# One rotation of four PSUM banks for up products and everything else in a two-branch transformer block

## The chip, the cores and the metric

The kernel runs on one core of one Trainium2 chip. The metric is device time in microseconds (us) of one execution. A core has a matmul engine (TensorE, PE in the profile, with its weight loads as PEld), VectorE (DVE), ScalarE (ACT), GpSimd (POOL) and SyncE (SP), which issues most DMAs. Each engine takes its instructions strictly in the order in which they stand in its queue, and waits on semaphores that other engines or DMAs raise. Matmul results land in PSUM, which has eight banks of 128 partitions x 512 fp32. A bank can be written again only when what it held has been read out by ACT or DVE.

## What is computed

Input x is 2048 tokens x 512. Two branches read it, and a gate mixes them:

```python
g = sigmoid((x * gate_w).sum(-1, keepdims=True))
q, k, v = split_heads(x @ wqkv)                      # 32 heads of 16
phi(t) = concat(softmax(t @ w_phi), softmax(-t @ w_phi))
kv, z  = phi(k)^T v, sum over tokens of phi(k)       # linear attention
a      = (phi(q) kv / (phi(q) z + 1e-6)) @ wo
b      = relu(x @ w1 + b1)**2 @ w2 + b2              # 512 -> 1792 -> 512
out    = g * a + (1 - g) * b
```

## The kernel before

**Numbers.** Each fp32 operand is split into a high part (`..h`, rounded to the matmul's fp32r type by ACT) and a low part (`..l`, the rest, by DVE): `split`, L59. A product is then three matmuls per 128 rows of contraction (`mm3`, L67: high x high, high x low, low x high), so a product of 128 x 512 outputs over a contraction of 512 is 12 matmuls of 512 columns, 4 at L69, 4 at L70 and 4 at L71.

**Blocks.** Tokens are taken in 4 blocks of 512 (`SB`), each of 4 chunks of 128. The hidden size is cut into 14 slices of 128, 7 per sweep, in 2 sweeps over the 4 blocks: 56 steps t. A step has an up product u (hidden slice x block, transposed, `up`, L312), an ACT relu, square and split (`hidden`, L303), and two steps later four down products d, one per chunk (`down`, L318), which accumulate over the 7 slices in the four banks of `ps_d`.

**Attention work between the steps.** The first sweep also computes keys k and values v of all chunks (`do_k`, L402, `do_v`, L408), whose 16 pairs add up the key sums `kvps` (`do_kv`, L413) in one bank. The second computes queries q, their features, transposes by DMA, the numerators `num` (`numer`, L265) and the attended rows `att`. Before keys and before queries, w_phi is folded into the weights, 16 small matmuls in pairs of four (`fold`, L139: `foldk`, `foldq`), whose result is split from PSUM into `wkh`, `wkl` (or `wqh`, `wql`). A table of slots (`at`, L469), two per step, says after which up or down products these pieces are issued in the program. From that program order, priorities and dependencies a scheduler sets each engine's queue before the run.

**PSUM before.** Four banks are `ps_d`. Two are `ps_u`, used alternately by up products. The last two, `ps_a` and `ps_b`, are taken in turn by `bank()` (L51) for folds, k, v, q, num, att and the transposed sums `kvt`. After the fourth key fold `do_fold` drops `ps_b` out of the turn (L331), because `do_kv` keeps the key sums there until `kv_done` (L428) puts it back: in that stretch k and v share the single bank `ps_a`. A k is read out of its bank by four DVE instructions (L200 to L203, `exps`), a v by one ACT copy (L411, `vext`), an up product by one ACT relu (L305), a fold by ACT (L61) and then DVE (L64).

**Loads.** SP issues the loads in program order. Weights and x pass through four staging buffers (`in`), each free again after its split. x rows for the gate (`row<-in_xn`, L171), the broadcast bias `b2b` (L473) and the gate weights `gwb` (L472) are loaded in the same queue.

Of the kernel before, what the change touches and what calls it, by code (L numbers as in the profile page):

```python
# [8 lines left out]
F32 = mybir.dt.float32  # L9
# [4 lines left out]
PSUM = bass.MemoryType.PSUM  # L14
DRAM = bass.MemoryType.DRAM

P = 128
S, D, H, DH, F = 2048, 512, 32, 16, 1792
NK = D // P
SB = 512  # L20
# [12 lines left out]
def tile_gated_mix(ctx: ExitStack, tc: tile.TileContext, xT, xn, wqT, wkT, wphi, wv, wo, w1, b1, w2, b2, gw, out):  # L33
    nc = tc.nc
    pool = lambda name, bufs, **kw: ctx.enter_context(tc.tile_pool(name=name, bufs=bufs, **kw))
# [6 lines left out]
    small = pool("small", 3)  # L42
    dram = pool("dram", 1, space=DRAM)
    ps_d = pool("ps_d", NC, space=PSUM)
    ps_u = pool("ps_u", 2, space=PSUM)
    ps_a = pool("ps_a", 1, space=PSUM)
    ps_b = pool("ps_b", 1, space=PSUM)
    banks = [ps_a, ps_b]
    taken = [0]

    def bank(name):  # L51
        p = banks[taken[0] % len(banks)]
        taken[0] += 1
        return p.tile([P, 512], F32, tag="s", name=name)
# [4 lines left out]
    def split(src, hi, lo, ehi, elo):  # L59
        if ehi is nc.scalar:  # L60
            i = nc.scalar.activation(hi, src, AF.Copy)  # L61
        else:
            i = ehi.tensor_copy(hi, src)
        elo.tensor_tensor(lo, src, hi.bitcast(F32), ALU.subtract)  # L64
        return i
# [11 lines left out]
    def load(src):  # L77
        t = stage.tile([P, 512], F32, tag="in", name="in")
        nc.sync.dma_start(t, src)
        return t  # L80

    def row():
        return work.tile([P, D], F32, tag="row", name="row", bufs=6)

    def ffn_tiles(nm, fc):
        return (fpool.tile([P, 512], F32R, tag=nm + "h", name=f"{nm}h{fc}"),
                fpool.tile([P, 512], F32R, tag=nm + "l", name=f"{nm}l{fc}"))
# [51 lines left out]
    def fold(loaded, nm, k):  # L139
        wph, *t = loaded  # L140
        ps = bank(f"fold{nm}{k}")
        for g in range(NK):
            nc.tensor.matmul(ps[:, g * P:(g + 1) * P], t[g][:, k * P:(k + 1) * P], wph[:, g * P:(g + 1) * P],
                             start=True, stop=True)
        hi = wpool.tile([P, 512], F32R, tag=f"wah{k}", name=f"w{nm}h{k}")
        lo = wpool.tile([P, 512], F32R, tag=f"wal{k}", name=f"w{nm}l{k}")
        with tc.high_priority(offset=AHEAD):
            split(ps, hi, lo, nc.scalar, nc.vector)
        return hi, lo
# [150 lines left out]
    def up_step(ps, k, xs, wf):  # L300
        st["up"] = mm3(ps, wf, xs[k], slice(k * P, (k + 1) * P), ALL, k == 0, k == NK - 1)

    def hidden(fc, ps):  # L303
        r = work.tile([P, SB], F32, tag="r", name="r")
        nc.scalar.activation(r, ps, AF.Relu, bias=b1c[:, fc:fc + 1])  # L305
        nc.scalar.activation(r, r, AF.Square)  # L306
        hh = work.tile([P, SB], F32R, tag="hh", name="hh", bufs=LAG + 1)
        hl = work.tile([P, SB], F32R, tag="hl", name="hl", bufs=LAG + 1)
        st["act"] = split(r, hh, hl, nc.scalar, nc.vector)
        return hh, hl  # L310

    def up(fc, xs, wf):  # L312
        ps = ps_u.tile([P, SB], F32, tag="u", name="u")
        for k in range(NK):
            up_step(ps, k, xs, wf)
        return hidden(fc, ps)
# [8 lines left out]
    def do_fold(nm, k):  # L325
        with tc.issue_after(st["up"].ins):
            st["wa", nm, k] = fold(st["wT"], nm, k)
        if k == NK - 1:
            st["wa"] = [st["wa", nm, i] for i in range(NK)]
            if nm == "k":  # L330
                banks.pop()  # L331

    def do_w(src, nm):
        st["wb"] = load_w(src, nm)
# [23 lines left out]
    def idle(n):  # L358
        for _ in range(n):
            st["up"] = nc.tensor.matmul(st["warm"], st["zeros"][:, :P], st["zeros"], start=True, stop=True)  # L360


    def start():
        t = row()
        hi, lo = up_w[0] = ffn_tiles("w1", 0)
        xs = st["x", 0] = []
        ps = ps_u.tile([P, SB], F32, tag="u", name="u")
        for k in range(NK):
            s = slice(0, P) if k == 0 else slice(P, 512)
            u = load(xT[0, :, k, :])  # L370
            if k == 0:
                for piece in (s, slice(P, 512)):
                    nc.scalar.dma_start(t[:, piece], w1[0][:, piece])
            xs.append((xpool.tile([P, SB], F32R, tag="xh", name=f"xh0_{k}"),
                       xpool.tile([P, SB], F32R, tag="xl", name=f"xl0_{k}")))
            if k == 0:
                split(t[:, s], hi[:, s], lo[:, s], nc.vector, nc.vector)
            nc.scalar.activation(xs[k][0], u, AF.Copy)
            low = nc.vector.tensor_tensor(xs[k][1], u, xs[k][0].bitcast(F32), ALU.subtract)
            if k == 0:  # L380
                rest_w = slice(P, 512)
                with tc.issue_after(low.ins):
                    split(t[:, rest_w], hi[:, rest_w], lo[:, rest_w], nc.vector, nc.gpsimd)
            (xh, xl), kk = xs[k], slice(k * P, (k + 1) * P)
            with tc.issue_after(st["up"].ins):
                st["up"] = nc.tensor.matmul(ps, hi[:, kk], xh, start=k == 0, stop=False)
            if k < 2:
                with tc.issue_after(st["up"].ins):
                    idle(2)
            with tc.issue_after(st["up"].ins):  # L390
                nc.tensor.matmul(ps, hi[:, kk], xl, start=False, stop=False)
                st["up"] = nc.tensor.matmul(ps, lo[:, kk], xh, start=False, stop=k == NK - 1)
            if k < 1:
                with tc.issue_after(st["up"].ins):
                    idle(2)
        st["u0"] = ps
# [81 lines left out]
    for k in range(NK):  # L478
        at(3 + k // 2, do_fold, "k", k)
    at(1, do_w, wv, "v")  # L480
    for b in range(NB):
        for c in range(NC):
            s = b * SL + 3 * c - 3 if b else 7 + c
# [3 lines left out]
        for c in range(NC):  # L487
            n = b * NC + c
            s = 5 + 2.9 * n
# [6 lines left out]
    for k in range(NK):  # L496
        at(49 + k, do_fold, "q", k)
# [7 lines left out]
    for p in range(NB * NC // 2):  # L505
        n, s = 2 * p, 54 + 6 * p
# [12 lines left out]
    def do_up(t):  # L519
        if t < len(work_list):  # L520
            sw, b, i = work_list[t]
            fc = sw * NFH + i
            hid[t] = up(fc, st["x", sw * NB + b], up_w[fc])

    warm_up()
    start()
    for fc in range(1, LAG + 1):
        do_w1(fc)
# [87 lines left out]
```

## Time and profile before

| | us |
|---|---|
| median of 3 runs | 531.09 |
| lowest, highest | 531.03, 531.55 |
| span of the profiled execution | 528.2 |

The span goes from the first to the last instruction of one profiled execution. The timed runs hold some 2.9 us more around it. In the timeline a row is: start us, length us, engine, line, operation, out<-in, matmul size, shape, count; in brackets stands the idle time before it and what ended it. A matmul's length overlaps the next one's, so the distance from one start to the next is what a matmul costs on a busy PE.

### The profile page before, as it was taken

How to read it: one execution, taken by the hardware profiler on the slowest of the kernel's cores; microseconds unless marked ns; L12 is line 12 of the kernel's file. 1: busy time of each engine (PE TensorE's matmuls, PEld its weight loads, DVE VectorE, ACT ScalarE, POOL GpSimd, SP SyncE). 2: the span in 40 equal slices, each digit the busy share in tenths (PEclk: the TensorE clock that was granted, in tenths of full speed). 3: DMA queues.
4: the chain of work that ended last, by engine and by line, in shares of the span. 5: the costliest groups of instructions: out<-in, count | busy, mean ns of one | idle time of the engine just before them, and what ended most of it. 6: DMA issues, size and time to landing. Idle time of an engine off the chain costs nothing.

```text
span 528.2 us, 8945 instructions
## 1 busy us (share of the span) xinstructions
PE 519.0 (98%) x3475; PEld 417.6 (79%) x3475; DVE 356.5 (68%) x608; ACT 234.1 (44%) x404; POOL 77.0 (15%) x61
## 2 busy tenths in 40 slices
PE   8998999999999999999999999999999999999997
PEld 4876888888888888888878878787887878787785
DVE  4688546833656334566769897998878887779423
ACT  4874424623335234354644663463435353535230
POOL 2001111111111111011103121102011111112000
PEclk9999999999999999999999999999999999999999
DMA  7974004200032000434346114134102311022102
GB/s 255 297 234 131 1 1 161 81 2 1 24 138 79 2 0 22 159 85 137 81 146 215 34 40 124 66 107 130 45 17 89 113 49 30 24 77 94 47 1 79
DMA packets 30834, 45.16 MB, mean 86 GB/s; under 512 B 5704, under 2 KB 12360, under 8 KB 30792
## 3 DMA queue, kind: packets, MB, share of 16 engines
q1 hardware_dynamic: 30328, 44.20, 26.8%
q8 instruction: 27, 0.44, 0.4%
q10 hardware_dynamic: 432, 0.39, 0.2%
q14 instruction: 15, 0.12, 0.1%
q0 software_dynamic: 32, 0.01, 0.0%
HBM read 29.89 MB, written 8.39 MB: 72 GB/s over the span
## 4 chain that ended last, share of the span: by engine, by line
PE 63%; DVE 15%; DMA 7%; ACT 5%; SPq 5%; issue 2%; POOL 2%; DVEq 0%; POOLq 0%; ACTq 0%
PE u L69 6%; PE u L71 6%; PE u L70 6%; PE d L71 6%; PE d L70 6%; PE d L69 6%; SPq L259 4%; PE k L69 3%; PE v L69 2%; PE k L70 2%; PE k L71 2%; PE v L70 2%; PE v L71 2%; DMA in<-in_w 2%; PE att L69 2%
## 5 line engine op out<-in xcount | busy, mean ns | idle before, releaser
L305 ACT ACTIVATE r<-u,b1c 128x512 f32<-128x512 f32 x56 | 38.5, 687 | 152.1 <-PE u L71 143.5
L69 PE MATMUL d<-w2h,hh 128*128 128x512 f32 x224 | 87.5, 390 | 0.0
L69 PE MATMUL u<-xh,w1h 128*128 128x512 f32 x220 | 86.8, 395 | 0.4 <-ACT w1h L61 0.4
L70 PE MATMUL d<-w2l,hh 128*128 128x512 f32 x224 | 87.2, 389 | 0.0
L71 PE MATMUL d<-w2h,hl 128*128 128x512 f32 x224 | 87.2, 389 | 0.0
L71 PE MATMUL u<-xh,w1l 128*128 128x512 f32 x220 | 85.8, 390 | 0.1
L70 PE MATMUL u<-xl,w1h 128*128 128x512 f32 x220 | 85.7, 390 | 0.0
L64 DVE TENSOR_TENSOR hl<-r,hh 128x512 fp32r<-128x512 f32 x56 | 42.8, 764 | 55.9 <-ACT hh L61 55.9
L233 POOL TENSOR_TENSOR ez<-e,z 128x512 f32<-128x512 f32 x32 | 41.4, 1316 | 187.7 <-ACT e L205 187.7
L214 POOL TENSOR_TENSOR e<-e,r 128x1024 f32<-128x1024 f32 x16 | 32.4, 2025 | 202.1 <-DVE r L210 144.8
L208 DVE TENSOR_REDUCE sm<-e 128x64 f32<-128x1024 f32 x32 | 39.0, 1217 | 28.5 <-ACT e L205 28.3
L69 PEld LDWEIGHTS u<-xh,w1h 128*128 128x128 f32 x220 | 41.3, 188 | 12.2 <-ACT hh L61 1.6
L71 PEld LDWEIGHTS d<-w2h,hl 128*128 128x128 f32 x224 | 42.1, 188 | 8.7
L69 PEld LDWEIGHTS d<-w2h,hh 128*128 128x128 f32 x224 | 42.0, 188 | 8.7
L70 PEld LDWEIGHTS d<-w2l,hh 128*128 128x128 f32 x224 | 42.1, 188 | 8.6
L71 PEld LDWEIGHTS u<-xh,w1l 128*128 128x128 f32 x220 | 41.3, 188 | 9.1 <-DVE w1l L64 0.6
L70 PEld LDWEIGHTS u<-xl,w1h 128*128 128x128 f32 x220 | 41.3, 188 | 8.2
L205 ACT ACTIVATE e<-e 128x1024 f32<-128x1024 f32 x32 | 33.8, 1055 | 23.2 <-DVE e L203 22.4
L257 ACT ACTIVATE phiT<-tb 32x256 f32<-32x256 f32 x64 | 26.4, 413 | 34.6 <-DVE tb L251 33.9
L61 ACT ACTIVATE hh<-r 128x512 fp32r<-128x512 f32 x56 | 35.2, 628 | 1.3
L306 ACT ACTIVATE r<-r 128x512 f32<-128x512 f32 x56 | 35.1, 627 | 1.0
L566 DVE SCALAR_TENSOR_TENSOR row<-d,rest,row 128x512 f32<-128x512 f32 (+1 forms) x33 | 22.4, 731 | 8.5 <-PE d L71 8.5
(106 smaller groups left out, 875.4 us busy)
## 6 DMA issues: line engine op xcount, KB each, us to landing
in<-in_xT SPq DMA_DIRECT2D x32, 256.0 KB, 3.8
in<-in_w SPq DMA_DIRECT2D x24, 256.0 KB, 3.1
phiT<-tb SPq DMA_DIRECT2D x192, 32.0 KB, 1.8
row<-in_xn SPq DMA_DIRECT2D x16, 256.0 KB, 2.8
part<-row SPq DMA_DIRECT2D x16, 256.0 KB, 2.0
row<-part SPq DMA_DIRECT2D x16, 256.0 KB, 3.7
out<-row SPq DMA_DIRECT2D x15, 256.0 KB, 2.3
row<-in_wkT SPq DMA_DIRECT2D x4, 256.0 KB, 5.8
```

What stands on the lines that cost most here:

```text
L61: i = nc.scalar.activation(hi, src, AF.Copy)
L64: elo.tensor_tensor(lo, src, hi.bitcast(F32), ALU.subtract)
L69: nc.tensor.matmul(o, ah[:, sa], bh[:, sb], start=first, stop=False)
L70: nc.tensor.matmul(o, ah[:, sa], bl[:, sb], start=False, stop=False)
L71: return nc.tensor.matmul(o, al[:, sa], bh[:, sb], start=False, stop=last)
L205: nc.scalar.activation(ef, ef, AF.Exp)
L208: nc.vector.tensor_reduce(sm, e3, AX.X, ALU.add)
L214: eng.tensor_tensor(e3, e3, w.unsqueeze(2).to_broadcast([P, 2 * H, DH]), ALU.mult)
L233: nc.gpsimd.tensor_tensor(ez[:, hs, :], e3[:, hs, :], zbc[half], ALU.mult)
L257: nc.scalar.activation(dst, src, AF.Copy)
L305: nc.scalar.activation(r, ps, AF.Relu, bias=b1c[:, fc:fc + 1])
L306: nc.scalar.activation(r, r, AF.Square)
```

## The change

The two up banks and the two banks of the rest become one list of four, `[ps_a, ps_b, ps_e, ps_f]`, and up products take theirs from `bank()` like everything else. The first up product, u of slice 0, is given `ps_e` outright and does not count in the turn. While the key sums hold `ps_b`, the list has three banks.

```diff
     ps_d = pool("ps_d", NC, space=PSUM)
-    ps_u = pool("ps_u", 2, space=PSUM)
-    ps_a = pool("ps_a", 1, space=PSUM)
-    ps_b = pool("ps_b", 1, space=PSUM)
-    banks = [ps_a, ps_b]
+    ps_a, ps_b, ps_e, ps_f = (pool(f"ps_{i}", 1, space=PSUM) for i in "abef")
+    banks = [ps_a, ps_b, ps_e, ps_f]
...
     def up(fc, xs, wf):
-        ps = ps_u.tile([P, SB], F32, tag="u", name="u")
+        ps = bank("u")
...
             if nm == "k":
-                banks.pop()
+                banks.remove(ps_b)
...
         xs = st["x", 0] = []
-        ps = ps_u.tile([P, SB], F32, tag="u", name="u")
+        ps = ps_e.tile([P, SB], F32, tag="s", name="u")
```

By the program order, takes 0 to 6 of the new turn are u1, u2, u3, foldk0, foldk1, foldk2, foldk3 in a, b, e, f, a, b, e. Then `ps_b` leaves, and take 7 modulo 3 is e again: u4 stands in the bank of foldk3. Takes 8 to 12 are k0 in f, u5 in a, v0 in e, k1 in f, u6 in a.

The scheduler answers with another order. On PE before, after the last key fold, u4 (here `u_429`, the product of `w1h4`) came whole, then the first key product (`k_455`):

```order
L143 MATMUL foldk3_396<-row_249,row_253 128x128
L69 MATMUL u_429<-xh0_0_136,w1h4_321 128x512 [waits Activation_49]
L70 MATMUL u_429<-xl0_0_137,w1h4_321 128x512
...
L71 MATMUL u_429<-xh0_3_173,w1l4_322 128x512
L69 MATMUL k_455<-wkh0_356,xh0_0_136 128x512 [waits DVE_49]
L70 MATMUL k_455<-wkl0_357,xh0_0_136 128x512
```

In the changed kernel (line numbers are two lower) the same place reads, with `u_432` for u4 and `k_458` for the key product:

```order
L141 MATMUL foldk3_399<-row_252,row_256 128x128
L67 MATMUL k_458<-wkh0_359,xh0_0_139 128x512 [waits DVE_49]
L68 MATMUL k_458<-wkl0_360,xh0_0_139 128x512
L69 MATMUL k_458<-wkh0_359,xl0_0_140 128x512
L67 MATMUL k_458<-wkh1_368,xh0_1_156 128x512 [waits Activation_49]
L68 MATMUL k_458<-wkl1_369,xh0_1_156 128x512 [waits DVE_49]
L69 MATMUL k_458<-wkh1_368,xl0_1_157 128x512
L67 MATMUL k_458<-wkh2_395,xh0_2_167 128x512 [waits Activation_49]
L67 MATMUL u_432<-xh0_0_139,w1h4_324 128x512 [waits DVE_49]
L68 MATMUL u_432<-xl0_0_140,w1h4_324 128x512
```

Seven matmuls of the key product moved ahead of u4, and u4 now begins with a wait for DVE.

On ACT, the queue before that serves this place, from the relu of u3 (`r_338`) to the fourth fold's high part `wkh3`, was:

```order
L305 ACTIVATE r_338<-u_325,b1c_98 128x512
L178 ACTIVATE ge_633<-lg_631 128x1
L306 ACTIVATE r_338<-r_338 128x512
L61 ACTIVATE wkh0_356<-foldk0_351 128x512
L61 ACTIVATE w1h4_321<-in_319 128x512
L61 ACTIVATE wkh1_365<-foldk1_360 128x512
...
L61 ACTIVATE xh1_0_407<-in_405 128x512
L178 ACTIVATE ge_688<-lg_686 128x1
L61 ACTIVATE wkh2_392<-foldk2_387 128x512
L61 ACTIVATE xh1_1_413<-in_411 128x512
L61 ACTIVATE wkh3_401<-foldk3_396 128x512
```

And in the changed kernel:

```order
L303 ACTIVATE r_341<-u_328,b1c_101 128x512
L59 ACTIVATE wkh0_359<-foldk0_354 128x512
L59 ACTIVATE w1h4_324<-in_322 128x512
L59 ACTIVATE wkh1_368<-foldk1_363 128x512
L304 ACTIVATE r_341<-r_341 128x512
L59 ACTIVATE w2h4_350<-in_348 128x512
...
L59 ACTIVATE xh1_0_410<-in_408 128x512
L176 ACTIVATE ge_636<-lg_634 128x1
L59 ACTIVATE wkh2_395<-foldk2_390 128x512
L59 ACTIVATE wkh3_404<-foldk3_399 128x512
```

The square of u3 (`r<-r`) moved behind `w1h4` and `wkh1`, and `wkh3` no longer stands behind `xh1_1`. DVE's low parts follow suit: before, they ran `w1l5`, `xl1_0`, `wkl2`, `xl1_1`, `wkl3`; now `w1l5`, `xl1_0`, `wkl2`, `wkl3`.

On SP, the load queue before, from the gate weights on, was:

```order
L472 DMA gwb<-in_gw 128x512
L171 DMA row<-in_xn 128x512
L79 DMA in<-in_wv 128x512 x4
L473 DMA b2b<-in_b 128x512
L171 DMA row<-in_xn 128x512
L79 DMA in<-in_w 128x512 x3
```

and is now:

```order
L470 DMA gwb<-in_gw 128x512
L471 DMA b2b<-in_b 128x512
L77 DMA in<-in_wv 128x512 x4
L169 DMA row<-in_xn 128x512
L77 DMA in<-in_w 128x512 x3
L77 DMA in<-in_xT 128x512
```

One of the two x rows that stood ahead of the three loads `in<-in_w` (the first of them is `w1h4`'s) moved behind them. Elsewhere PE's queue differs at a few more places by one to four matmuls or a whole fold, among them the first up products (two matmuls of u2 ahead of the rest of u0 and u1), the second key product (now whole ahead of the down products that it used to interrupt), and the query folds; from the first query product on, no engine's order changes.

## The prediction

> **What bounds the kernel now.** I read the page first, for which engine is full; then PE's own waits, for what still interrupts it; then PE's timeline at those waits, since distances between starts show what a busy share hides; then ACT's, DVE's and SP's timelines around the one place where the change can add a wait.
>
> ```profile
> span 528.2 us, 8945 instructions
> PE 519.0 (98%) x3475; PEld 417.6 (79%) x3475; DVE 356.5 (68%) x608; ACT 234.1 (44%) x404; POOL 77.0 (15%) x61
> PEclk9999999999999999999999999999999999999999
> ...
> PE k L69 <- ACT vext L411: 1.1, 1, 1.1
> PE num L270 <- DMA phiT<-tb: 1.1, 2, 0.6
> PE kvt L444 <- DVE row L433: 0.4, 1, 0.4
> PE v L69 <- DVE e L203: 0.3, 1, 0.3
> PE foldk L143 <- DVE wkl L64: 0.2, 1, 0.2
> ```
>
> PE is busy for 98% at full clock (9 is 90% or more), and no other engine comes near. The change removes no matmul, so the most it can bring is PE's waits. They are few and short; the list gives total us, times, longest. Three of them, k, v and foldk, wait for something that was reading a PSUM bank. num and kvt wait for data (transposed features, key sums copied out), which no bank helps.
>
> What a matmul costs without a wait:
>
> ```profile
> 32.30 0.39 PE L69 MATMUL k<-wkh,xh 128*128 128x512 f32 x1
> ...
> 35.02 0.39 PE L69 MATMUL d<-w2h,hh 128*128 128x512 f32 x1
> ```
>
> Twelve matmuls in 2.72 us are 0.227 each. Whatever lies between two starts beyond 0.227 is lost time, including the first matmul after a wait, whose successor follows later than usual.
>
> **What goes: the waits for a bank.** The rows at the four places:
>
> ```profile
> 22.46 1.95 PE L143 MATMUL foldk<-row 128*128 128x128 f32 x16
> 24.16 0.48 PE L69 MATMUL d<-w2h,hh 128*128 128x512 f32 x1
> ...
> 26.75 0.39 PE L71 MATMUL d<-w2h,hl 128*128 128x512 f32 x1
> 27.35 2.36 PE L143 MATMUL foldk<-row 128*128 128x128 f32 x16 [0.21 <-DVE wkl L64]
> 29.46 0.48 PE L69 MATMUL u<-xh,w1h 128*128 128x512 f32 x1
> ...
> 40.23 0.39 PE L71 MATMUL u<-xh,w1l 128*128 128x512 f32 x1
> 40.95 0.47 PE L69 MATMUL v<-wvh,xh 128*128 128x512 f32 x1 [0.34 <-DVE e L203]
> 41.26 0.40 PE L70 MATMUL v<-wvl,xh 128*128 128x512 f32 x1
> ...
> 44.44 0.39 PE L69 MATMUL d<-w2h,hh 128*128 128x512 f32 x1
> 45.92 0.50 PE L69 MATMUL k<-wkh,xh 128*128 128x512 f32 x1 [1.09 <-ACT vext L411]
> 46.26 0.40 PE L70 MATMUL k<-wkl,xh 128*128 128x512 f32 x1
> ...
> 242.84 0.39 PE L71 MATMUL d<-w2h,hl 128*128 128x512 f32 x1
> 243.37 0.50 PE L69 MATMUL k<-wkh,xh 128*128 128x512 f32 x1
> 243.71 0.40 PE L70 MATMUL k<-wkl,xh 128*128 128x512 f32 x1
> ```
>
> - Folds: the second pair starts 26.75 to 27.35, 0.60, so 0.37 late, and takes 29.46 - 27.35 = 2.11 where the first took 24.16 - 22.46 = 1.70. Together 0.78. Both its banks still held the first pair. In the new turn they are b and e, which held u2 and u3, read out before.
> - First v: 0.72 - 0.227 = 0.49 late, and 0.08 for the successor: 0.57. It waits for the last DVE read of the first k, both in `ps_a`. Now it stands in e, k in f.
> - Second k: 1.48 - 0.227 = 1.25, and 0.11: 1.36. It waits for the copy of v out of `ps_a`. Now k1 needs f, left by k0 long before.
> - A last k: 0.53 - 0.227 = 0.30, and 0.11: 0.41. The same pair of tiles, at a time when ACT is late. With three banks it is gone.
>
> The sum is 3.12.
>
> **What comes: u4 behind a fold.** Take 7 gives u4 the bank of foldk3, which ACT and then DVE must read out. PE cannot pass a waiting matmul: the rest of k0, the down products and everything after stand behind u4. When is the bank free? The rows of before:
>
> ```profile
> 26.33 0.63 ACT L61 ACTIVATE w1h<-in 128x512 fp32r<-128x512 f32 x1 [0.61 <-DMA in<-in_w]
> 26.87 0.58 ACT L61 ACTIVATE wkh<-foldk 128x512 fp32r<-128x512 f32 x1
> 27.34 0.62 ACT L61 ACTIVATE hh<-r 128x512 fp32r<-128x512 f32 x1
> ...
> 28.38 0.62 ACT L61 ACTIVATE w1h<-in 128x512 fp32r<-128x512 f32 x1
> 28.90 0.62 ACT L61 ACTIVATE xh<-in 128x512 fp32r<-128x512 f32 x1
> 29.52 0.58 ACT L61 ACTIVATE wkh<-foldk 128x512 fp32r<-128x512 f32 x1
> ...
> 29.61 0.69 DVE L64 TENSOR_TENSOR w1l<-in,w1h 128x512 fp32r<-128x512 f32 x1
> 30.21 0.69 DVE L64 TENSOR_TENSOR xl<-in,xh 128x512 fp32r<-128x512 f32 x1
> ```
>
> Call T the start of the ACT copy `w1h4`, which waits for its DMA: 26.33 before. ACT then runs back to back, 0.52 a copy (28.38 to 28.90). The square that moved in delays w1h5 by 0.52, from 28.38 to 28.90, done 29.52. On DVE four passes now follow it, 0.60 apart (29.61 to 30.21): w1l5 at 29.6, xl at 30.2, wkl2 at 30.8, wkl3 at 31.4, done 0.69 later. ACT isn't the later one: wkh2 starts at 29.52 + 0.52 = 30.04, wkh3 0.47 after it (as 26.87 to 27.34) and ends 0.58 later, at 31.09. So u4 starts at about 32.12 if T stays, T + 5.8 in general.
>
> Without any loss against before it would start at 29.46 + 7 x 0.227 = 31.05, with the seven matmuls of k0 now ahead. With T as before the place is 1.07 + 0.11 for the restart = 1.18 later. This already contains the 0.78 that the folds gain: PE comes sooner and waits longer, because the end of the wait hangs on ACT and DVE.
>
> Does T stay? It hangs on a DMA.
>
> ```profile
> 19.76 0.43 SPq L473 DMA_DIRECT2D b2b<-in_b  x1
> 20.64 0.33 SPq L171 DMA_DIRECT2D row<-in_xn  x1
> 21.83 1.37 SPq L79 DMA_DIRECT2D in<-in_w  x2
> ...
> 20.00:22.00 2.00, 2.00 (x10) 1.65 (x9) 1.31 (x3) 1.55 (x3) 0.00 (x0) 1.00 0.87 287
> ...
> 24.47 0.19 ACT L178 ACTIVATE ge<-lg 128x1 f32<-128x1 f32 x1
> ```
>
> The load of w1h4 is issued at 21.83 behind b2b and an x row, with the DMA engines 87% busy at 287 GB/s (last columns). Now only one 256 KB transfer stands there: 0.26 MB / 287 GB/s = 0.91 sooner. Against it, u0 ends a little later, because two matmuls of u2 stand in it: up to 2 x 0.227, and the chain from u0's relu to these loads with it, at most 0.45. The earliest T is 24.94, one fold copy (0.47) after the gate's exponential leaves 24.47 free. I take 25.75, near the DMA's end of this, since its queue is full there. Then u4 loses 1.18 - 0.58 = 0.60. The ends: T = 26.78 loses 1.63; T = 24.94 gains 0.21.
>
> **Everything else.** For every other tile, set when its new bank's last tile is read out in the trace of before against when it is first written. The u behind the first query fold would be too early, but the new order puts a v and a fold between them. The tightest after that is this:
>
> ```profile
> 424.23 0.68 DVE L203 TENSOR_TENSOR e<-mn,q 128x512 f32<-128x512 f32 x1
> ...
> 426.14 0.50 PE L69 MATMUL u<-xh,w1h 128*128 128x512 f32 x1
> ```
>
> The last read of a q ends at 424.91 and the u that gets its bank starts at 426.14, 1.23 of cover: nothing is paid unless DVE runs that much later. The two x rows, the other moved loads, ACT's and DVE's small gate instructions lie beside a PE that doesn't wait for them: nothing. The tail after PE's last matmul is untouched.
>
> **The sum** from u4 on: +0.60 (folds included) - 0.57 - 1.36 - 0.41 = -1.74. With the ends of T: -0.71 to -2.55. The profiled execution would go from 528.2 to 526.5; the median, 2.9 above the span, from 531.1 to 529.4.
>
> The Trainium skill, "Perfetto Trace Analysis", section Optimizing Tensor Performance, Matmuls, says that independent groups should rotate through different banks so that one's evacuation overlaps the next one's matmuls. Read alone it speaks for the whole 3.12 (528.0), which is beyond rival 2 below and shares its chance; the rows say that this turn itself puts u4 on an occupied bank.
>
> **Rivals.**
>
> 1. *The gain is eaten* (no change, 531.0). Either T is late and the place costs all of 1.63, or the waits for data at kvt (0.4) and num (1.1 in the list above) grow by what PE gains, because PE only arrives sooner at a DMA that lands when it did. Half of my gain lost gives 530.3, all but 0.1 gives 531.0. Against it: kvt's and num's data come from k and q products that PE itself computes after the gain. For it: the gain is only 1.7, and the u4 term spans 1.8.
> 2. *The fold's bank is free in time* (faster, 528.6): T at 24.94, -2.55. ACT has to find w1h4 landed by then, 3.1 after its issue, with the queue still busy.
> 3. *The idle PE loses its clock* (slower, 533). If b2b, now ahead of the values' weights, holds up the later loads instead, T moves up. For no gain at all T must be 1.16 beyond before, 27.5; PE then waits from about 30.3 to 33.3. A wait of that size hasn't occurred: the longest in the list is 1.1. What an unready clock costs stands at the start:
>
> ```profile
> 1.19 4.88 PE L360 MATMUL warm<-zeros 128*128 128x512 bf16 x11 [1.19 <-DVE zeros L354]
> ```
>
> Eleven warm-up matmuls of the same 512 columns took 4.88, 0.44 each, 0.22 over the later pace: 2.4 in all. With the gain gone, that is 531.1 + 2.4 = 533.5; a partial drop gives 533. It decides from T = 27.5 on. The Trainium skill, "TensorE: Matmul & The Clock Gate", section Why this matters for your kernels, warns of a clock halved after idle gaps over some 3 us; no run here shows such a drop in the middle.
>
> **How the numbers follow.** A difference under 0.2% (1.06 us) can't be told from none. Forecast: 0.60, at 529.4, own range 528.6 to 530.4. Rival 1: 0.24, 530.4 to 531.4. Rival 2: 0.10. Rival 3: 0.06. A fifteenth of the forecast's chance (0.04) lies above 530.03, so faster is 0.56 + 0.10 = 0.66, same 0.04 + 0.24 = 0.28, slower 0.06. The range 528.4 to 531.1 leaves out rival 3, the upper part of rival 1 and what lies a little below rival 2.
>
> **What would show it.** In the changed profile, PE's waits should no longer name k, v and foldk; one wait of u for `wkl` should appear near 30 us, 1 to 2 long, the seventh matmul of k0 just before it. Before 22 us PE should shift by at most 0.5. T, the ACT copy `w1h` before the second `wkh`, should lie near 25.8. At 243 the k should follow the d by 0.23. kvt's wait and num's should stay at 0.4 and 1.1. I am wrong if u4 waits beyond 2.5, if other tiles wait for banks in the key stretch, or if the gain at 50 us is missing again at 300.

## The result and the profile after

| us | before | changed |
|---|---|---|
| median of 6 runs each, side by side | 531.06 | 528.24 |
| lowest, highest | 530.70, 532.08 | 527.30, 530.23 |
| span of the profiled execution | 528.2 | 526.7 |
| that execution's own time | not taken | 528.44 |

The ratio is 0.9948, 95% interval 0.9928 to 0.9968: 2.8 us faster. The forecast was 1.7 faster (529.4), and the time lies 0.16 below the range. The direction held; the size didn't.

The changed kernel's page, its span, engines and granted clock, and behind them PE's waits (total us, times, longest):

```profile
span 526.7 us, 8947 instructions
PE 517.0 (98%) x3475; PEld 417.9 (79%) x3475; DVE 357.4 (68%) x608; ACT 234.4 (45%) x404; POOL 77.2 (15%) x61
```

```profile
PE num L268 <- DMA phiT<-tb: 1.1, 2, 0.6
PE u L67 <- DVE wkl L62: 1.1, 1, 1.1
PE kvt L442 <- DVE row L431: 0.9, 1, 0.9
...
PE att L69 <- DVE ol L62: 0.4, 1, 0.4
PE k L67 <- ACT wkh L59: 0.3, 1, 0.3
```

The bank waits of before (k for `vext`, v for `e`, foldk for `wkl`) are gone, and a u waits for `wkl`, the DVE read of a key fold. That is u4. PE's timeline around it:

```profile
29.75 0.39 PE L69 MATMUL k<-wkh,xl 128*128 128x512 f32 x1
...
30.39 0.50 PE L67 MATMUL k<-wkh,xh 128*128 128x512 f32 x1 [0.26 <-ACT wkh L59]
31.96 0.50 PE L67 MATMUL u<-xh,w1h 128*128 128x512 f32 x1 [1.06 <-DVE wkl L62]
32.30 0.40 PE L68 MATMUL u<-xl,w1h 128*128 128x512 f32 x1
```

ACT's and DVE's rows behind these waits, in the changed kernel:

```profile
25.86 0.63 ACT L59 ACTIVATE w1h<-in 128x512 fp32r<-128x512 f32 x1 [0.84 <-DMA in<-in_w]
...
29.76 1.07 ACT L59 ACTIVATE wkh<-foldk 128x512 fp32r<-128x512 f32 x2
```

```profile
27.01 0.69 DVE L62 TENSOR_TENSOR wkl<-foldk,wkh 128x512 fp32r<-128x512 f32 x1 [0.89 <-ACT wkh L59]
...
29.42 0.69 DVE L62 TENSOR_TENSOR w1l<-in,w1h 128x512 fp32r<-128x512 f32 x1
30.02 0.68 DVE L62 TENSOR_TENSOR xl<-in,xh 128x512 fp32r<-128x512 f32 x1
30.63 1.28 DVE L62 TENSOR_TENSOR wkl<-foldk,wkh 128x512 fp32r<-128x512 f32 x2
```

The chain is the one forecast: T (the copy `w1h4`) at 25.86 after a DMA, `wkh2` and `wkh3` as one pair on ACT, then on DVE `xl` and the two `wkl`, done at 30.63 + 1.28 = 31.91, and u4 at 31.96, 6.10 after T. Between the starts 30.39 and 31.96 lie 1.57, so 1.34 over the pace of 0.227; the successor adds 0.11.

In the kernel before, DVE began the same run of passes with the low part of `w1h4`:

```profile
27.21 0.68 DVE L64 TENSOR_TENSOR w1l<-in,w1h 128x512 fp32r<-128x512 f32 x1
```

That was 0.88 after its T of 26.33. In the changed kernel a `wkl` stands first and waits for ACT's `wkh`, so the run begins at 27.01, 1.15 after T.

Later places of the changed kernel, then the same in the kernel before:

```profile
423.28 1.09 PE L268 MATMUL num<-phiT,kvb 64*32 64x256 f32 x32
...
430.10 0.39 PE L68 MATMUL att<-wol,oh 128*128 128x512 f32 x1
430.91 0.50 PE L69 MATMUL att<-woh,ol 128*128 128x512 f32 x1 [0.43 <-DVE ol L62]
```

```profile
424.40 1.81 PE L270 MATMUL num<-phiT,kvb 64*32 64x256 f32 x32
...
431.50 0.39 PE L71 MATMUL d<-w2h,hl 128*128 128x512 f32 x1
432.01 0.50 PE L69 MATMUL att<-woh,oh 128*128 128x512 f32 x1
```

At 242 the last k follows the d after 0.22 (241.85 to 242.07), without the wait that the first profile of before has there (what became of it stands below). At 423 stands something that the prediction doesn't have: the same 32 matmuls of num take 1.09 where they took 1.81. PE was held up inside them before, and no row of the list of PE's waits said so. PE's weight loads in the kernel before show where:

```profile
425.09 0.64 PEld L270 LDWEIGHTS num<-phiT,kvb 64*32 64x32 f32 x30 [0.55 <-issue]
```

They stop after the first two of 32 and go on at 425.09, 0.18 after the end of the q's last read (424.23 + 0.68 = 424.91) that the prediction quotes. A part of it comes back at the attended rows: before, they began 0.51 after the last d, 0.28 over the pace; now the third of them comes 0.81 after the second, 0.58 over.

### The profile page after: what moved, and what is told of

It reads as the page before. It is cut to its first block, busy times and chain, and to the rows that moved or that the text cites. A ratio compares the mean times of both kernels' runs of the same rounds, so it can differ in the third digit from the quotient of the medians.

```text
span 526.7 us, 8947 instructions
## 1 busy us (share of the span) xinstructions
PE 517.0 (98%) x3475; PEld 417.9 (79%) x3475; DVE 357.4 (68%) x608; ACT 234.4 (45%) x404; POOL 77.2 (15%) x61
## 4 chain that ended last, share of the span: by engine, by line
PE 73%; DVE 11%; SPq 5%; DMA 4%; ACT 3%; issue 2%; POOL 2%; DVEq 0%; ACTq 0%; POOLq 0%
PE u L67 7%; PE u L68 7%; PE u L69 7%; PE d L67 7%; PE d L69 7%; PE d L68 7%; SPq L257 4%; PE v L67 3%; PE v L68 3%; PE v L69 3%; PE k L69 3%; PE k L68 3%; PE k L67 3%; PE att L69 2%; POOL ez L231 2%
## 5 line engine op out<-in xcount | busy, mean ns | idle before, releaser
L62 DVE TENSOR_TENSOR hl<-r,hh 128x512 fp32r<-128x512 f32 x56 | 39.3, 702 | 55.7 <-ACT hh L59 55.7
```

## Experiments

The theory: the gain is the stretch of keys and values, less u4's wait, and the rest (some 1 us more than forecast) comes from the num at 424 and from a first profile of before that wasn't typical. The rivals: the query side carries the gain; or each wait that goes pays for itself, so that the folds alone bring 0.78.

To compare executions I use the start of the same matmul in PE's timeline, less its start in the first profile of before (at each place the median over 13 neighbouring matmuls). So the difference of two columns is what a kernel won (minus) or lost between them.

| execution (its span) | 26 us | 49 | 240 | 262 | 420 | 433 | end |
|---|---|---|---|---|---|---|---|
| before, first (528.2) | 0 | 0 | 0 | 0 | 0 | 0 | 0 |
| before, second (529.2) | 0.04 | 0.32 | 0.32 | 0.47 | 0.94 | 0.98 | 1.01 |
| before, third (529.6) | -0.22 | 1.33 | 1.39 | 1.29 | 1.31 | 1.35 | 1.36 |
| four banks from the queries on (527.9) | 0.24 | -0.14 | -0.07 | -0.19 | 0.11 | -0.34 | -0.31 |
| folds alone (528.9) | -0.11 | 0.39 | 0.47 | 0.57 | 0.59 | 0.63 | 0.67 |
| changed (526.7) | -0.16 | -1.02 | -1.00 | -1.63 | -1.12 | -1.56 | -1.53 |
| changed again (525.8) | -0.17 | -1.57 | -1.55 | -2.19 | -2.04 | -2.48 | -2.39 |
| key stretch alone (527.5) | -0.27 | -0.30 | -0.12 | -0.76 | -0.71 | -0.70 | -0.70 |
| keys and values alone (526.6) | 0.49 | -0.68 | -0.64 | -1.28 | -1.23 | -1.68 | -1.62 |
| u4 in the free bank (524.3) | -0.12 | -2.89 | -2.86 | -3.49 | -3.48 | -3.93 | -3.87 |

### The kernel before, twice more

No edit: how much of a profile is one execution's own? With the profile that the prediction used, these are the first, the second and the third execution of before.

> The kernel before, unchanged, for the span of every execution. Theory A (the profiled execution of before was a short one): time less span is 1.74 us in every execution, as it was for the changed kernel (528.44 - 526.7), so the spans of before lie around 529.3 and the span 528.2 read for the prediction is at the low end; the trace shows the waits for a bank larger than the 3.1 us that I summed. Theory B (the time outside the span differs): the spans lie around 528.2 and 2.9 us lie outside them, 1.2 more than with the changed kernel.

> A third profile of the kernel before. Theory A: span 528.8 to 530, with waits for a bank at v, the second k and the query folds that differ from those of the other two profiles by some tenths each and sum to more than 3.1. Theory B (what differs is outside PE's waits): the same 3.1 and a longer span for another reason.

Measured: 531.43 against 531.13 (ratio 1.0008, 1.0000 to 1.0016), its profiled execution 530.98 with a span of 529.2; the third execution 531.33 with a span of 529.6. Time less span is 1.78 and 1.73 here, and lies between 1.72 and 1.85 in every execution of these experiments, so the first profile's 528.2 belongs to a run of some 530.0 (an estimate: 528.2 + 1.78), 1.1 below the median. That is what theory A expected. What differs between the executions, PE of the second and of the third:

```profile
41.26 0.47 PE L69 MATMUL v<-wvh,xh 128*128 128x512 f32 x1 [0.83 <-DVE e L203]
...
243.16 0.39 PE L71 MATMUL d<-w2h,hl 128*128 128x512 f32 x1
243.39 0.39 PE L69 MATMUL k<-wkh,xh 128*128 128x512 f32 x1
...
248.83 0.39 PE L69 MATMUL d<-w2h,hh 128*128 128x512 f32 x1
249.57 1.13 PE L143 MATMUL foldq<-row 128*128 128x128 f32 x8 [0.35 <-PE d L69]
```

```profile
27.85 2.36 PE L143 MATMUL foldk<-row 128*128 128x128 f32 x16 [0.94 <-DVE wkl L64]
...
42.25 0.47 PE L69 MATMUL v<-wvh,xh 128*128 128x512 f32 x1 [1.12 <-DVE e L203]
```

The second k's wait is the same in all three (1.09, 1.07, 1.06): from the start of v to that of k are 4.97 us each time. The first v's is 0.34, 0.83, 1.12, and the second pair of folds starts 0.37, 0.14 and 1.09 late. The late k of the first execution doesn't wait in the other two (0.23 after the d); the query fold behind it is late there instead, by 0.51 and 0.26. Added up as in the prediction, with the query fold in the late k's place, the waits for a bank come to 3.12 in the first, 0.55 + 1.08 + 1.34 + 0.58 = 3.55 in the second and 1.51 + 1.36 + 1.33 + 0.34 = 4.54 in the third (folds, first v, second k, query fold).

The first v hangs on DVE's last read of k0; DVE and ACT of the third execution:

```profile
36.38 0.69 DVE L64 TENSOR_TENSOR xl<-in,xh 128x512 fp32r<-128x512 f32 x1 [0.95 <-ACT xh L61]
...
41.43 0.68 DVE L203 TENSOR_TENSOR e<-mn,k 128x512 f32<-128x512 f32 x1
```

```profile
35.72 0.63 ACT L61 ACTIVATE xh<-in 128x512 fp32r<-128x512 f32 x1 [1.01 <-DMA in<-in_xT]
```

The read ends at 42.11 and v starts 0.14 later, at 42.25. In the second execution it ended at 41.12 (v at 41.26), in the first at 40.81 (v at 40.95). In the third, DVE stood idle for a load of x whose copy on ACT starts at 35.72, against 34.59 in the first: 1.13 of the 1.30 by which the read is late. So there a DMA's landing decides how long PE stands at v. In the second execution that copy starts at 34.66, only 0.07 later; most of the 0.31 by which its read is late arises at a DVE pass over a gate row (38.02 against 37.72), and what held that one the profile doesn't name.

### The key stretch alone

The changed kernel, in which from `kv_done` on up products and the rest have two banks each again:

```diff
+    ups = [0]
+    apart = []
...
     def up(fc, xs, wf):
-        ps = bank("u")
+        if apart:
+            p = (ps_e, ps_f)[ups[0] % 2]
+            ups[0] += 1
+            ps = p.tile([P, SB], F32, tag="s", name="u")
+        else:
+            ps = bank("u")
...
-        banks.append(ps_b)
+        banks[:] = [ps_a, ps_b]
+        apart.append(1)
```

> The changed kernel up to the end of the key sums; from then on up products take ps_e and ps_f in turn and everything else ps_a and ps_b, as before. Theory A: the key stretch holds nearly all of the gain, and the query stretch only the 0.7 that num1 waits for a bank at 424 us less what att then gives back: 0.3 over the changed kernel, 528.5, so 2.5 under before. Rival (the query stretch holds the missing 1.1 us of the gain): 529.4.

Measured: 528.89 against 531.13, ratio 0.9962 (0.9947 to 0.9976): 2.0 us by the ratio, of the changed kernel's 2.8. The interval (528.3 to 529.9) holds both theory A's 528.5 and the rival's 529.4, so the time alone doesn't tell them apart; the profile does. PE's waits and its timeline at 424:

```profile
PE k L69 <- ACT wkh L61: 1.1, 1, 1.1
...
PE u L69 <- DVE wkl L64: 1.0, 1, 1.0
```

```profile
423.69 1.80 PE L270 MATMUL num<-phiT,kvb 64*32 64x256 f32 x32
```

u4's wait is there, 6.10 after a late T of 26.57, and the num takes 1.80 again, as before. In the table this execution wins nothing between 420 and 433, and 0.64 between 240 and 262 like every kernel with the new turn of the keys.

### Four banks from the queries on

The other half: before's two pairs until `kv_done` (near 270 us), then all four banks in turn. The order on every engine is that of before.

```diff
+    ups = [1]
+    joined = []
...
     def up(fc, xs, wf):
-        ps = ps_u.tile([P, SB], F32, tag="u", name="u")
+        if joined:
+            ps = bank("u")
+        else:
+            p = (ps_e, ps_f)[ups[0] % 2]
+            ups[0] += 1
+            ps = p.tile([P, SB], F32, tag="s", name="u")
...
-        banks.append(ps_b)
+        banks[:] = [ps_a, ps_b, ps_e, ps_f]
+        joined.append(1)
```

> The kernel before up to the end of the key sums, every engine's order as before throughout; from then on all four banks are taken in turn by everything. Theory A: 0.3 under before, 530.7 (the wait of num1 at 424 us goes, 0.7, and att gives 0.4 back). Rival (the query stretch holds the missing 1.1): 529.9 to 529.6. If no bank binds there: 531.0.

Measured: 530.95, ratio 0.9995 (0.9984 to 1.0005), not told from none; the rival's 529.9 lies outside the interval. PE at 424 and at the attended rows:

```profile
424.51 1.09 PE L270 MATMUL num<-phiT,kvb 64*32 64x256 f32 x32
...
432.13 0.50 PE L71 MATMUL att<-woh,ol 128*128 128x512 f32 x1 [0.41 <-DVE ol L64]
```

With nothing changed but the banks, num's 1.81 becomes 1.09: 0.72 won, less 0.3 at the attended rows. In the table that is 0.45 between 420 and 433, the same as in the changed kernel (0.44). So num there was waiting for a bank, not for data.

Up to `kv_done` this kernel is the kernel before, so the first part of its profile is one more execution of that one, and again a short one: 529.66, the lowest of its twelve, with a first v that waits 0.17. Its last k doesn't wait either, and a query fold at 248 is 0.27 late instead.

### Folds alone

Before's order on every engine; the four key folds get four banks, keys and values stay in the single one.

```diff
-        ps = bank(f"fold{nm}{k}")
+        ps = ((ps_a, ps_b, ps_e, ps_f)[k].tile([P, 512], F32, tag="s", name=f"foldk{k}") if nm == "k"
+              else bank(f"fold{nm}{k}"))
...
+    ups = [ps_f, ps_e, ps_f, ps_b]
...
-        ps = ps_u.tile([P, SB], F32, tag="u", name="u")
+        p = ups.pop(0) if len(ups) else (ps_e, ps_f)[fcs[0] % 2]
+        fcs[0] += 1
+        ps = p.tile([P, SB], F32, tag="s", name="u")
```

> The kernel before, every engine's order as before, in which only the four key folds get a bank each (u3 and u4 make room; u4 takes the bank of foldk1). Theory A (each wait for a bank is a term of its own, as I summed them): the 0.37 before the second pair of folds and the 0.41 inside it go, 0.78 under before, 530.4. Rival C (the waits stand in a row, and PE that comes sooner to v waits longer for k0's bank, whose last read hangs on DVE): the wait of v at 40 us grows by what the folds gain, and the time stays at 531.1.

Measured: 531.44, ratio 1.0002 (0.9988 to 1.0017). PE's folds and first v:

```profile
26.86 1.95 PE L144 MATMUL foldk<-row 128*128 128x128 f32 x16
...
41.33 0.47 PE L68 MATMUL v<-wvh,xh 128*128 128x512 f32 x1 [1.61 <-DVE e L204]
```

The second pair of folds waits no more, and v waits 1.61, where it waited 0.34 to 1.12 in the three executions of before. PE came to v sooner, and v starts 0.14 after DVE's last read of k0, as before (41.33, inside the 40.95 to 42.25 of before). That is what rival C expected. The 0.78 of the folds (a ratio of 0.9985, just outside the interval) didn't show in the time: two waits in a row on one chain were one wait.

### Keys and values alone

The changed kernel, with the folds back in two banks and u4 in a free one. Up to the second key product at 43 us the order on every engine is that of before again:

```diff
-        ps = bank(f"fold{nm}{k}")
+        ps = ((ps_a, ps_b)[k % 2].tile([P, 512], F32, tag="s", name=f"foldk{k}") if nm == "k"
+              else bank(f"fold{nm}{k}"))
...
+    ups = [ps_f, ps_e, ps_f, ps_e]
...
-        ps = bank("u")
+        p = ups.pop(0) if ups else None
+        ps = p.tile([P, SB], F32, tag="s", name="u") if p else bank("u")
...
                 banks.remove(ps_b)
+                taken[0] = 2
```

> The changed kernel, in which the key folds use two banks in turn as before and u4 has a free one; from k0 on the changed kernel's turn. Theory A with the waits as read from the one profile of before: v 0.57, second k 1.36, the late k 0.41 and num1 0.3 go, 2.6 under before, 528.5. Theory A with larger typical waits (0.5 more at v and 0.5 at the query folds, as in the second profile of before): 3.2 to 3.6 under before, 527.6. Rival C: the folds' 0.78, kept, is what is left of the gain in no other kernel, and 528.5 or more.

Measured: 527.82, ratio 0.9939 (0.9923 to 0.9954); the changed kernel on the same chip, run again without an edit, 528.40, ratio 0.9962 (0.9946 to 0.9978). Against before that is 3.2 by the ratio and by the medians, nearest to theory A with the larger typical waits. Rival C's 528.5 lies just inside the interval (526.9 to 528.6). One row of this kernel's list of PE's waits:

```profile
PE foldk L143 <- DVE wkl L63: 1.0, 1, 1.0
```

The folds' own wait in place of u4's is at least not worse; the two intervals overlap, so that it is better isn't shown.

> The changed kernel again, for a second profile and more executions on the chip of the others. Theory A: u4 starts 5.8 to 6.1 after the ACT copy w1h4, whatever that is, so the span moves with that copy; median 528.2 to 528.8, spans 1.74 under the times. Rival (the gain is in the kernel before's first measurements only): 529.4, as forecast.

In that second execution u4 starts at 31.39, 6.11 after a T of 25.28, and the span is 525.8. Span less u4's start is 494.7, 494.4 and 494.8 in the changed kernel, its repeat and the key stretch alone: what u4's chain loses early stays lost, within 0.4, to the end.

### u4 in the free bank

The changed kernel with one line more, which moves the turn on by one, so that u4 gets the bank of the first fold, not of the last:

```diff
                 banks.remove(ps_b)
+                taken[0] += 1
```

> The changed kernel with one place of the turn left out when ps_b leaves it, so that u4 takes the bank of foldk0 (ps_f) and not that of foldk3; u4 then stands whole ahead of k0 again. Theory A: the wait of u4 (1.34 and 0.11 for the restart) and the one of k0's seventh matmul for wkh2 (0.42) go, 1.87 in all, and some of that comes back at kvt: 526.4 to 527.0, 1.2 to 1.9 under the changed kernel. Rival (the gain is eaten): kvt, whose wait grew from 0.56 to 1.06 in the changed kernel, takes nearly all of it, 528.0.

Measured: 526.18 (526.09 to 527.02), ratio 0.9915 (0.9902 to 0.9929): 4.5 us under before by the ratio, 4.9 by the medians (531.13), and 2.1 under the changed kernel's median (1.8 by the two ratios); the fastest of all, a little below theory A's 526.4. The end of the list of PE's waits and its timeline where u4 waited:

```profile
PE att L69 <- DVE ol L62: 0.4, 1, 0.4
PE kvt L443 <- DVE row L432: 0.4, 1, 0.4
```

```profile
26.85 1.95 PE L141 MATMUL foldk<-row 128*128 128x128 f32 x16
28.55 0.48 PE L67 MATMUL u<-xh,w1h 128*128 128x512 f32 x1
```

The sixteen matmuls of the last two folds run in one piece and u4 follows at once, whole, ahead of k0: the order on PE moved with the bank. From there to the transposed key sums PE waits for no bank. The Trainium skill, "Perfetto Trace Analysis", section Optimizing Tensor Performance, Matmuls, says to rotate independent groups through banks so that reading one out overlaps the next one's matmuls. This pair of kernels agrees, with a condition: by the same number of banks the turn leaves a wait of 1.06 or none, and some 2 us between them, according to which old tile the next one meets.

## Why the prediction was wrong in its size

**Wrong: the basis.** "The profiled execution would go from 528.2 to 526.5; the median, 2.9 above the span, from 531.1 to 529.4." The changed kernel's spans are 526.7 and 525.8, and its median stands for one of 526.5 (528.24 - 1.78). The span was forecast rightly; the step from the span to the median, by 2.9, is what failed. Only 1.72 to 1.85 lies around a span, so the 2.9 that stands with the profile before is wrong too. The other 1.1 was the kernel's own, which the first profiled execution happened not to pay: its waits for a bank come to 3.12 where the second and third have 3.55 and 4.54, and its kvt waits 0.40 where the second's waits 0.82. "First v: 0.57" was right for that execution and about half of what the others pay (1.08 and 1.36), and what is added to a median has to come from an execution that costs as much as the median's.

**The terms**, against that first execution, place by place in the changed kernel's row of the table (its repeat behind it): -1.02 (-1.57) at 49 us, forecast 0.60 - 0.57 - 1.36 = -1.33; then -0.61 (-0.62) up to 262, forecast -0.41; +0.51 (+0.15) up to 420, forecast 0; -0.44 (-0.44) up to 433, forecast 0; then +0.03 (+0.09). In all -1.53 (-2.39), forecast -1.74. That this comes so near is partly luck, since terms are wrong on both sides:

- **u4, 0.60.** T was taken at 25.75 and came at 25.86 (25.28 in the repeat). u4 was put at T + 5.8 and came at T + 6.10 (6.11). Its place costs 31.96 - 31.05 + 0.11 = 1.02, and 0.45 in the repeat (31.39): the mechanism was right, the size hangs on the landing of one DMA, as the ends of the forecast said. The 0.30 beyond T + 5.8 is mostly DVE's: "w1l5 at 29.6" left that pass where it was before, 3.28 after T, but it came at 29.42, 3.56 after T, because the run of passes that leads up to it now begins with a `wkl` that waits for ACT.
- **The late k, -0.41.** Between 240 and 262 us all five profiles with the new turn of the keys win 0.63 or 0.64. But the k's own wait belongs to the first execution: in the four other profiles with before's banks there (second, third, folds alone, four banks from the queries on) the k follows the d after 0.23, and the query fold behind it is 0.26 to 0.51 late instead. One of the two waits costs each of them 0.3 to 0.6; in the new turn there is neither. So the size was nearly right and the place was one execution's. The rest of the gain lies at the query folds too, where the order on PE changed together with the banks; which of the two brings it wasn't tried.
- **"num and kvt wait for data (transposed features, key sums copied out), which no bank helps", and with it "Everything else", at nothing.** This step failed. The two listed waits of num are for data and stayed at 1.1, and kvt's is for data too. A third num, at 424.40, waited inside its 32 matmuls, which the list didn't show; its own row (1.81, against 1.09) did, and its weight loads go on 0.18 after the last read of a q ends. In the kernel before a num takes both banks of the rest, so one of them is the q's. I looked for places where the new turn makes a bank late and for waits that the list names, not for groups that take longer than their like, though I quoted the read of the q at 424.23 that ends just there. Worth 0.72, less some 0.3 at the attended rows: the -0.44, shown by the kernel with four banks from the queries on.
- **kvt's wait, to stay at 0.4,** was 0.9 here, 0.5 in the repeat and 0.4 in three other kernels with the change's turn; before had 0.4, 0.8 and 0.4. Its 0.9 belongs to one execution.

**Against before's usual execution.** The mean of its three at the end is 0.79, of the changed kernel's two -1.96: 2.75 apart, the medians 2.82. By place the difference is -1.85 up to 49 us, -0.65 up to 262, +0.17 up to 420, -0.47 up to 433, +0.05 after it. The profiles with before's queue there differ by 1.47 at 49 us alone (-0.14 to 1.33), so how the -1.85 divides between v, the second k, the folds and chance stays open.

**Rivals.** The gain was not eaten (rival 1): num's listed waits stayed at 1.1, kvt's (0.9 and 0.5) lie near the 0.4 to 0.8 of before, and only the one at the attended rows grew, by 0.3. That rival was right of another edit, the folds alone. The fold's bank did not come free in time (rival 2), but its price is now known: with u4 in a free bank some 2 more are won, where I had 0.8 for an early T and 1.4 for no such wait at all.

Rival 3 was not seen in the profiles: PE stood idle for 1.06 at u4, the granted clock there is 1.00, and T stayed below 27.5 in every profile with u4's wait. The warm-up row that priced it doesn't show a lowered clock either: the granted clock is 1.00 from the first microsecond on in that trace. But six of the changed kernel's eighteen timed executions have a mean granted clock of 0.995 to 0.997 and take 529.12 to 531.19, while the other twelve have 0.998 or more and take 527.30 to 528.74; in the kernel before it is one of 59 (0.997). No such execution was profiled, so where the clock dropped, and whether u4's wait has to do with it, stays open. The kernel with the key stretch alone has that wait too, and none of its six executions lies below 0.998.

## What to carry to other kernels

Waits in a row on one chain don't add up: taking the first (folds alone, 0.78 of wait removed) moved it into the next and gained nothing, taking all of them, and the num's, gained 4.5 to 4.9. In a shared turn of buffers, look for the one tile that meets the slowest reader, and shift the turn by one: here one line was worth some 2 us, with the order that the scheduler made of it. And when a profile's waits hang on DMA landings, find out how its execution stands to the median before adding its sum to it; and compare the lengths of like groups, because a list of waits leaves stalls out.

## What was not expected of the hardware

Three profiled executions of one kernel differ by 1.4 us in the span (528.2, 529.2, 529.6). In the third most of it arises before 49 us, where loads, staging copies and bank waits meet: there it is 1.33 behind the first, and 1.36 at the end. The second is 0.32 behind there and loses 0.69 more later, most of it at the query folds and at kvt. The two kernels in which u4 has a free bank had the narrowest spreads (526.09 to 527.02 in five runs, 527.49 to 528.35 in six; the changed one 527.30 to 530.23 in six), and none of their runs has a mean granted clock below 0.999.

The granted clock falls to 0.50 only after the last matmul: in the changed kernel that one starts at 522.39, the clock is 1.00 up to 524 us, 0.88 on average in the next microsecond and 0.50 after it. PE's longest idle time between the warm-up and there, 1.06 at u4, leaves it at 1.00.
